# Four feed-forward blocks computed ahead instead of five, with key-sum products and tail remainders moved from VectorE to GpSimd

## The chip, the cores and the metric

The kernel runs on one core of a Trainium2 chip. The metric is the device time of one execution in microseconds. Before the change three runs gave 1642.47, 1645.51 and 1647.66 us; their median is 1645.51 us. The engines are named as in the profile: PE is TensorE (PEld its weight loads), DVE is VectorE, ACT is ScalarE, POOL is GpSimd, SP is SyncE, which here only issues DMAs. A name with q (SPq, POOLq) is that engine's instruction sequencer.

## The reference, cut to what matters

The input x has 2048 rows of 576 numbers in fp32. It is normalised and goes two ways: through a linear attention with 32 heads of 18, and through a gated feed-forward net of width 4608, whose output gates the attention's.

```python
xn = _layernorm(x)                                    # 2048 x 576
q, k, v = split(xn @ wqkv)                            # 32 heads of 18
phi_q = concat(softmax(q @ w_phi), softmax(-(q @ w_phi)))   # phi_k alike
kv = einsum("bhsf,bhsd->bhfd", phi_k, v);  z = einsum("bhsf->bhf", phi_k)
o = einsum("bhqf,bhfd->bhqd", phi_q, kv) / (einsum("bhqf,bhf->bhq", phi_q, z) + 1e-6)
s = o @ wo
g = silu((silu(xn @ w_gate) * (xn @ w_up)) @ w_down)
out = x + s * g
```

All products are made to nearly full fp32 precision: each operand is split into a high part in a reduced fp32 format and a low remainder, and three of the four partial products are added up. ACT casts the high part (line 58) and an elementwise engine subtracts it for the remainder (line 59), so each split costs two elementwise passes.

## The kernel before, in words

The feed-forward width is cut into NF = 36 **F blocks** of 128. The rows of x stay in on-chip memory, transposed, as eight tiles X of 512 columns in two halves (i = 0, 1) of 1024 rows. The work has these stages, told with their places in the profile:

- **Preparation** (0 to about 70 us): load, normalise, transpose and split x, fold w_phi into the query and key weights. 
- **Key stage** (about 70 to 226 us): for each of 16 row tiles, the softmaxes of the keys and the state kv with the key sums z as an extra column, summed in three PSUM banks `kvp` of four, four and two states.
- **Turn to the queries** (lines 492 to 515): ACT copies the ten columns of key sums one at a time from `kvp` into `zc`. Ten small matmuls spread each over 128 rows in PSUM, and four ACT copies gather them in `zb` (lines 501 to 509). Then, for each of the ten states, DVE multiplies by a block mask and the result is split into KVH and KVL (lines 510 to 515).
- **Query stage** (about 226 to 485 us, lines 523 to 636): eight steps of 256 rows. A step has two `q_tile` (projection `pq`, its two softmaxes, and the denominator), one `numer` (transposes of e, product with the states) and one `project` (product with wo, stored to `s_dram`). In `q_tile` DVE multiplies e by `zb` into `ez` (line 568, 1152 columns) and sums by head into y (line 570); y gives the denominator that scales e on line 577. The first use of the buffer `ez` is as a landing place for the last rows of wo (lines 529 to 532), which `split_wo` splits.
- **Tails** (lines 542 to 555, eight calls spread over the query stage): small sums of the last 64 rows of the gate and up weights for later; POOL makes four differences, ACT the high part, DVE the remainder (line 552), and POOL issues twelve DMAs per call to `t_dram`.
- **Main stage** (about 513 us to the end, `gate_up`, line 727 and on): for each half i and each F block not computed ahead, gate and up projections by Strassen's scheme: seven products of seven matmuls (line 706), 512 columns each, which is 49 matmuls per block and half. The down projections (line 805) are interleaved, from a queue that `fill` serves. At its start `operands(0)` loads the row sums that the scheme needs, four tiles of 1280 KB, into the places of x's second half.

The **F blocks computed ahead** (f < EARLY = 5) are made from x directly by `early_tile` (lines 113 to 124), without the scheme: per half two pairs (j = 0, 1) of 2 x 14 matmuls of 512 columns on line 92 (tile `pe`), with a Silu on ACT (line 119) and a product on DVE (line 122). Their result h is stored to `h_dram`, and read back in the main stage by `stored` in place of a `gate_up`. A block is four pairs in all. Two blocks' second halves are made in the preparation, one pair at the end of the key stage, the other pairs of f = 0 to 3 in the query stage as filler between the query's own matmuls, and all of block EARLY - 1 after it (lines 994 to 1000): half 1 before `operands(0)` and half 0 behind it.

The order on each engine is fixed when the kernel is built: a scheduler places each instruction by its place in the program, by what it depends on, and by hints (`high_priority`, `issue_after`). On the chip each engine takes its instructions in that order. `tails(n)` is hinted to come after the e of query tile 3n/2 + 2. In the main stage `units` puts the stored blocks at the places 4f + 1 (first half) and 4f (second half) of the 36.

Of the kernel before, what the change touches and what calls it, by code (L numbers as in the profile page):

```python
# [9 lines left out]
F32 = mybir.dt.float32  # L10
# [3 lines left out]
AX = mybir.AxisListType  # L14
# [3 lines left out]
P = 128  # L18
# [7 lines left out]
GW = GH * DH  # L26
GROUPS = [(g * GW, min(GW, D - g * GW)) for g in range((D + GW - 1) // GW)]
NG = len(GROUPS)
QS = 256
EARLY = 5  # L30
TAILS = (NF - EARLY + 3) // 4
LAG = 3
RUSH = NF - 5
# [4 lines left out]
def heads(ap):  # L38
    return ap.rearrange("p (h d) -> p h d", d=DH)
# [7 lines left out]
def gated_hedgehog_kernel(ctx: ExitStack, tc, x, w_qk, w_v, w_phi, wo, w_gu, w_tail, w_down, ident_in, mask_in, out):  # L47
# [9 lines left out]
    def split(hi, lo, src):  # L57
        nc.scalar.copy(hi, src)  # L58
        nc.vector.tensor_sub(lo, src, hi)  # L59
# [66 lines left out]
    with ExitStack() as att:  # L126
# [364 lines left out]
        with ExitStack():  # L491
            qc = att.enter_context(tc.tile_pool(name="qc", bufs=1, reuse_waits="tile"))
            KVH = qc.tile([GW, 2 * NG, GW], F32R, name="KVH")
            KVL = qc.tile([GW, 2 * NG, GW], F32R, name="KVL")
            zb = qc.tile([P, 2 * D], F32, name="zb")
            zc = qc.tile([GW, 2 * NG], F32, name="zc")
            for i in range(3):
                for j in range(4 if i < 2 else 2):
                    w = GROUPS[(4 * i + j) // 2][1]
                    nc.scalar.copy(zc[0:w, 4 * i + j:4 * i + j + 1], kvp[i][0:w, j, w:w + 1])  # L500
            for s in range(2):
                for a, m, name in ((0, 4, ("p2", "vw")[s]), (4, 1, ("vy", "vx")[s])):
                    o, w = GROUPS[a]
                    zp = kps.tile([P, 512], F32, name=name)
                    for g in range(a, a + m):
                        nc.tensor.matmul(zp[:, (g - a) * GW:(g - a) * GW + w],
                                         zc[0:w, 2 * g + s:2 * g + s + 1].to_broadcast([w, P]), ident[0:w, 0:w],
                                         start=True, stop=True)
                    nc.scalar.copy(zb[:, s * D + o:s * D + o + m * w], zp[:, 0:m * w])
            for i in range(2 * NG):  # L510
                o, w = GROUPS[i // 2]
                km = qc.tile([GW, GW], F32, name="km", bufs=2)
                nc.vector.tensor_mul(km[0:w, 0:w], kvp[i // 4][0:w, i % 4, 0:w],
                                     mask.rearrange("p h d -> p (h d)")[0:w, 0:w])
                split(KVH[0:w, i, 0:w], KVL[0:w, i, 0:w], km[0:w, 0:w])

        raw_x(order[7], 0, 1)
        raw_x(order[7], 2, 3)
# [4 lines left out]
        with ExitStack() as qst:  # L523
# [3 lines left out]
            WOH = qw.tile([GW, NG, D], F32R, name="WOH")  # L527
            WOL = qw.tile([GW, NG, D], F32R, name="WOL")
            wrs = [qk.tile([P, 2, D], F32, name="oh", bufs=1), qk.tile([P, 2, D], F32, name="ol", bufs=1),
                   qk.tile([P, 2, D], F32, name="ez", bufs=1)]  # L530
            for g, (o, w) in enumerate(GROUPS):
                nc.sync.dma_start(wrs[g // 2][0:w, g % 2], wo[o:o + w, :])

# [8 lines left out]
            def tails(n):  # L542
                t = qk.tile([P, 7, P], F32, name="tl", bufs=2)
                hi = qk.tile([P, 7, P], F32R, name="th", bufs=1)
                nc.sync.dma_start(t[:, 0:4], w_tail[n])
                sub = nc.gpsimd.tensor_sub
                sub(t[:, 4], t[:, 2], t[:, 0])
                sub(t[:, 2], t[:, 3], t[:, 2])
                sub(t[:, 5], t[:, 3], t[:, 4])
                sub(t[:, 6], t[:, 1], t[:, 5])  # L550
                nc.scalar.copy(hi, t)
                nc.vector.tensor_sub(t, t, hi)
                for b, src in enumerate((hi.bitcast(F32), hi.bitcast(F32), t)):
                    for q in range(4):
                        nc.gpsimd.dma_start(t_dram[n, q, b], src[32 * q:32 * q + 32])

            last_e = []

            def q_tile(t):
                i0, j0, cols = block(t)  # L560
                pq = qps.tile([P, 2, 512], F32, name="p2")
                for i in range(2):
                    w = slice(i * HALF, (i + 1) * HALF)
                    xw(pq[:, i, 0:HALF], i0, j0, cols, QH[:, :, :, w], QL[:, :, :, w], True)
                e = qk.tile([P, 2 * D], F32, name="e", bufs=4)
                r = softmax_parts(pq, e)
                ez = qk.tile([P, 2 * D], F32, name="ez", bufs=1)
                nc.vector.tensor_mul(ez, e, zb)
                y = qk.tile([P, 2 * H], F32, name="y")
                nc.vector.reduce_sum(y, heads(ez), axis=AX.X)  # L570
                nc.vector.tensor_mul(y, y, r)
                den = qk.tile([P, H], F32, name="den")
                nc.vector.scalar_tensor_tensor(den, y[:, 0:H], DEN_EPS, y[:, H:], op0=ALU.add, op1=ALU.add)
                nc.vector.reciprocal(den, den)
                nc.vector.tensor_mul(r.rearrange("p (s h) -> p s h", s=2), r.rearrange("p (s h) -> p s h", s=2),
                                     den.unsqueeze(1).to_broadcast([P, 2, H]))
                last_e.append(nc.vector.tensor_mul(heads(e), heads(e), spread(r, 2 * H)))
                return e
# [498 lines left out]
```

## Time and profile before

| what | value |
|---|---|
| median of three runs | 1645.51 us |
| the profiled execution's own time | 1645.38 us |
| its span, first to last instruction | 1643.6 us |
| outside the span | 1.8 us |
| instructions | 25222 |
| bytes moved by DMA | 268.47 MB, 163 GB/s on average |

The page of a profile gives busy times of the engines over the whole span. The windows view gives the same for stretches that are named in us from the span's start: of each engine the busy time and, in brackets, the instructions. Groups of instructions are told by line, engine, operation, out<-in by the program's tile names and shape, then the count, the total busy time, the mean of one in ns, and the idle time of the engine just before them with what ended it. The chain of waits follows the work that ended last back to the start. A matmul's duration in a row is longer than its share of the engine, since matmuls overlap: the pace is read from a stretch of many.

### The profile page before, as it was taken

Reading aid. Unit: us, or ns where it says so; the run is one execution under the profiler, and the core shown is the slowest. Engines: PE = TensorE matmul, PEld = TensorE weight load, DVE = VectorE, ACT = ScalarE, POOL = GpSimd, SP = SyncE. Lnnn points to the kernel's source line nnn. Section 1 sums busy time; section 2 is a strip of 40 time slices with the busy share of each in tenths; the row PEclk is TensorE's granted clock in tenths of the full one; section 3 lists DMA queues with packets and bytes.
Section 4 is the critical chain, followed back from the end, with each engine's and each line's share of the span. In section 5 each row is a group of like instructions: output and inputs, shape, how many; then the busy total and the mean of one; then the engine's idle time right before and its main releaser. Section 6 shows DMA issues by size and latency. Waiting matters only on the chain.

```text
span 1643.6 us, 25222 instructions
## 1 busy us (share of the span) xinstructions
PE 1606.3 (98%) x9385; PEld 1428.2 (87%) x9385; DVE 1173.2 (71%) x1733; ACT 723.1 (44%) x1407; POOL 655.0 (40%) x699
## 2 busy tenths in 40 slices
PE   6999999999999999999999999999999999999997
PEld 5899987999987788888888888888888888888886
DVE  7667768989862678788777788825566766666578
ACT  5533344454432554454444444445433433333334
POOL 3385661433213455355445365313243324133132
PEclk9999999999999999999999999999999999999999
DMA  9522243433239545555545554685454655555445
GB/s 293 197 79 78 88 133 114 119 109 110 79 108 329 183 162 172 182 171 177 174 167 181 178 176 156 222 299 157 134 159 138 199 183 172 168 180 182 139 114 173
DMA packets 121741, 268.47 MB, mean 163 GB/s; under 512 B 12786, under 2 KB 53362, under 8 KB 119826
## 3 DMA queue, kind: packets, MB, share of 16 engines
q1 hardware_dynamic: 106652, 246.49, 45.8%
q0 software_dynamic: 3072, 11.02, 2.5%
q10 hardware_dynamic: 11894, 9.35, 1.8%
q8 instruction: 74, 1.21, 0.3%
q14 instruction: 49, 0.40, 0.1%
HBM read 167.19 MB, written 99.61 MB: 162 GB/s over the span
## 4 chain that ended last, share of the span: by engine, by line
PE 66%; DVE 2%; DMA 1%; issue 1%; POOL 0%; ACT 0%; SPq 0%; DVEq 0%; ACTq 0%
PE pd L805 24%; PE px L706 24%; PE pw L706 12%; PE py L706 6%; PE pe L92 1%; DVE acc L777 0%; DVE w L59 0%; DMA rb<-in_B_w_down 0%; DMA ld<-in_B_w_gu 0%; DVE hh L59 0%; DMA X<-s_dram 0%; DVE dw L59 0%; DVE ha L766 0%; DVE acc L778 0%; DVE s L740 0%
## 5 line engine op out<-in xcount | busy, mean ns | idle before, releaser
L805 PEld LDWEIGHTS pd<-dw,hh 128*128 128x128 f32 x3048 | 433.6, 189 | 25.5 <-DVE dw L59 2.0
L805 PE MATMUL pd<-dw,hh 128*128 128x288 f32 x3048 | 449.7, 297 | 3.2 <-DVE dw L59 1.5
L706 PE MATMUL px<-X,w 128*128 128x512 f32 x1488 | 385.9, 393 | 2.1 <-ACT w L58 1.3
L706 PEld LDWEIGHTS px<-X,w 128*128 128x128 f32 x1488 | 270.2, 188 | 55.5 <-ACT s L735 4.0
L706 PE MATMUL pw<-X,w 128*128 128x512 f32 x744 | 191.8, 393 | 0.0
L706 PEld LDWEIGHTS pw<-X,w 128*128 128x128 f32 x744 | 139.1, 188 | 31.2 <-DVE s L740 0.3
L740 DVE TENSOR_TENSOR s<-pw,s 128x512 f32<-128x512 f32 x124 | 85.3, 688 | 103.2 <-ACT s L735 91.7
L930 DVE TENSOR_TENSOR acc<-pd,acc 128x576 f32<-128x576 f32 x128 | 96.3, 753 | 85.3 <-PE pd L805 85.1
L735 ACT COPY s<-px 128x512 f32<-128x512 f32 x124 | 72.6, 586 | 160.0 <-PE px L706 159.9
L92 PE MATMUL pe<-X,wh 128*128 128x512 f32 (+1 forms) x380 | 121.4, 401 | 5.3 <-ACT h L119 2.2
L58 ACT CAST hh<-ha 128x512 fp32r<-128x512 f32 x140 | 82.7, 619 | 92.9 <-PE pd L805 72.6
L59 DVE TENSOR_TENSOR hh<-ha,hh 128x512 fp32r<-128x512 f32 x140 | 109.9, 811 | 18.1 <-ACT hh L58 17.1
L902 POOL TENSOR_TENSOR hb<-hb 128x512 f32<-128x512 f32 x34 | 46.7, 1372 | 161.9 <-DVE hb L762 161.5
L59 DVE TENSOR_TENSOR w<-ld,w 128x512 fp32r<-128x512 f32 (+1 forms) x93 | 79.6, 858 | 37.6 <-ACT w L58 36.3
L706 PE MATMUL py<-X,w 128*128 128x512 f32 x372 | 97.7, 396 | 1.1 <-ACT py L747 1.1
L706 PE MATMUL px<-X,wt 96*128 96x512 f32 x248 | 97.9, 395 | 0.0
L915 POOL TENSOR_TENSOR ha<-ha 128x512 f32<-128x512 f32 x34 | 52.6, 1563 | 104.0 <-DVE hh L59 104.0
L889 POOL TENSOR_TENSOR h<-ha,hb 128x512 f32<-128x512 f32 x34 | 44.9, 1321 | 123.2 <-DVE ha L766 90.1
L58 ACT CAST w<-ld 128x512 fp32r<-128x512 f32 (+1 forms) x93 | 50.9, 549 | 90.1 <-POOL ld L696 58.0
L92 PEld LDWEIGHTS pe<-X,wh 128*128 128x128 f32 (+1 forms) x380 | 69.9, 189 | 20.6 <-DVE h L122 3.4
L693 POOL TENSOR_TENSOR ts<-ld 128x256 f32<-128x256 f32 x31 | 27.3, 880 | 140.7 <-issue 70.0
L747 ACT COPY py<-px 128x512 f32<-128x512 f32 x62 | 35.5, 572 | 103.7 <-PE px L706 84.4
(262 smaller groups left out, 3238.1 us busy)
## 6 DMA issues: line engine op xcount, KB each, us to landing
w_dram<-w SPq DMA_DIRECT2D x90, 512.0 KB, 2.9
w<-w_dram SPq DMA_DIRECT2D x90, 512.0 KB, 4.5
wt<-t_dram SPq DMA_DIRECT2D x61, 336.0 KB, 3.6
ld<-in_B_w_gu SPq DMA_DIRECT2D x31, 512.0 KB, 4.5
X<-sum_dram SPq DMA_DIRECT2D x8, 1280.0 KB, 11.4
rt<-in_B_w_down SPq DMA_DIRECT2D x33, 288.0 KB, 3.0
rb<-in_B_w_down SPq DMA_DIRECT2D x33, 288.0 KB, 4.3
w_dram<-w SPq DMA_DIRECT2D x30, 256.0 KB, 2.2
```

Of the source, the lines that this page charges most:

```text
L58: nc.scalar.copy(hi, src)
L59: nc.vector.tensor_sub(lo, src, hi)
L92: last = nc.tensor.matmul(ps, l, r, start=n == 0, stop=n == len(pairs) - 1)
L706: nc.tensor.matmul(ps, l, r, start=first and n == 0, stop=last and n == len(mm) - 1, skip_group_check=True)
L735: nc.scalar.copy(t, ps)
L740: nc.vector.tensor_add(t, ps, t)
L747: nc.scalar.copy(yp, xp)
L805: nc.tensor.matmul(ps, l, r, start=first and n == 0 and m == 0, stop=n == len(hs) - 1 and m == 2, skip_group_check=True)
L889: sub(s, g["h"][0][0], g["h"][0][1])
L902: nc.gpsimd.tensor_add(a21, a21, g["h"][1][1])
L915: sub(a12, a12, g["h"][0][0])
L930: nc.vector.tensor_add(a2, pd[:, :, 0:HALF], a2)
```

## The change

EARLY falls from 5 to 4, so one F block (four pairs of line 92) is no longer computed ahead and goes through `gate_up` in both halves of the main stage. Four edits in and ahead of the query stage go with it. (1) `ez` is made by POOL in two halves of 576 columns with a buffer each, and DVE sums each half by head. (2) The remainder of the tails is subtracted by POOL instead of DVE, and a tails call issues three DMAs of 128 rows, two from ACT and one from SP, instead of twelve of 32 rows from POOL. (3) The key sums are copied by bank, three ACT copies for ten and two gathering copies for four. (4) The states are masked and split by bank, three times for ten.

```diff
-EARLY = 5
+EARLY = 4
...
-            zc = qc.tile([GW, 2 * NG], F32, name="zc")
-            for i in range(3):
-                for j in range(4 if i < 2 else 2):
-                    w = GROUPS[(4 * i + j) // 2][1]
-                    nc.scalar.copy(zc[0:w, 4 * i + j:4 * i + j + 1], kvp[i][0:w, j, w:w + 1])
-            for s in range(2):
-                for a, m, name in ((0, 4, ("p2", "vw")[s]), (4, 1, ("vy", "vx")[s])):
-                    o, w = GROUPS[a]
-                    zp = kps.tile([P, 512], F32, name=name)
-                    for g in range(a, a + m):
-                        nc.tensor.matmul(zp[:, (g - a) * GW:(g - a) * GW + w],
-                                         zc[0:w, 2 * g + s:2 * g + s + 1].to_broadcast([w, P]), ident[0:w, 0:w],
-                                         start=True, stop=True)
-                    nc.scalar.copy(zb[:, s * D + o:s * D + o + m * w], zp[:, 0:m * w])
-            for i in range(2 * NG):
-                o, w = GROUPS[i // 2]
-                km = qc.tile([GW, GW], F32, name="km", bufs=2)
-                nc.vector.tensor_mul(km[0:w, 0:w], kvp[i // 4][0:w, i % 4, 0:w],
-                                     mask.rearrange("p h d -> p (h d)")[0:w, 0:w])
-                split(KVH[0:w, i, 0:w], KVL[0:w, i, 0:w], km[0:w, 0:w])
+            zc = qc.tile([GW, 12], F32, name="zc")
+            m4 = mask.rearrange("p h d -> p (h d)")
+            banks = [(i, 4 if i < 2 else 2, GROUPS[2 * i][1]) for i in range(3)]
+            for i, n, w in banks:
+                nc.scalar.copy(zc[0:w, 4 * i:4 * i + n], kvp[i][0:w, 0:n, w])
+            zp, zq = kps.tile([P, 2, 512], F32, name="p2"), kps.tile([P, 512], F32, name="vw")
+            for g, (o, w) in enumerate(GROUPS):
+                for s in range(2):
+                    d = zp[:, s, o:o + w] if g < NG - 1 else zq[:, s * w:s * w + w]
+                    nc.tensor.matmul(d, zc[0:w, 2 * g + s:2 * g + s + 1].to_broadcast([w, P]), ident[0:w, 0:w],
+                                     start=True, stop=True)
+            z2, o = zb.rearrange("p (s n) -> p s n", s=2), GROUPS[-1][0]
+            nc.scalar.copy(z2[:, :, 0:o], zp[:, :, 0:o])
+            nc.scalar.copy(z2[:, :, o:D], zq[:, 0:2 * (D - o)].rearrange("p (s n) -> p s n", s=2))
+            for i, n, w in banks:
+                km = qc.tile([GW, 4, GW], F32, name="km")
+                nc.vector.tensor_mul(km[0:w, 0:n, 0:w], kvp[i][0:w, 0:n, 0:w],
+                                     m4[0:w, 0:w].unsqueeze(1).to_broadcast([w, n, w]))
+                split(KVH[0:w, 4 * i:4 * i + n, 0:w], KVL[0:w, 4 * i:4 * i + n, 0:w], km[0:w, 0:n, 0:w])
...
-                   qk.tile([P, 2, D], F32, name="ez", bufs=1)]
+                   qk.tile([P, D], F32, name="ez", bufs=2).unsqueeze(1)]
...
-                nc.vector.tensor_sub(t, t, hi)
+                sub(t, t, hi)
                 for b, src in enumerate((hi.bitcast(F32), hi.bitcast(F32), t)):
-                    for q in range(4):
-                        nc.gpsimd.dma_start(t_dram[n, q, b], src[32 * q:32 * q + 32])
+                    (nc.scalar, nc.scalar, nc.sync)[b].dma_start(t_dram[n, :, b], src)
...
-                ez = qk.tile([P, 2 * D], F32, name="ez", bufs=1)
-                nc.vector.tensor_mul(ez, e, zb)
                 y = qk.tile([P, 2 * H], F32, name="y")
-                nc.vector.reduce_sum(y, heads(ez), axis=AX.X)
+                for s in range(2):
+                    ez = qk.tile([P, D], F32, name="ez", bufs=2)
+                    nc.gpsimd.tensor_mul(ez, e[:, s * D:(s + 1) * D], zb[:, s * D:(s + 1) * D])
+                    nc.vector.reduce_sum(y[:, s * H:(s + 1) * H], heads(ez), axis=AX.X)
```

## The prediction

> **What bounds the kernel now.** First the page: the busy shares and the chain of work that ended last.
>
> ```profile
> PE 1606.3 (98%) x9385; PEld 1428.2 (87%) x9385; DVE 1173.2 (71%) x1733; ACT 723.1 (44%) x1407; POOL 655.0 (40%) x699
> PE 66%; DVE 2%; DMA 1%; issue 1%; POOL 0%; ACT 0%; SPq 0%; DVEq 0%; ACTq 0%
> ```
>
> PE is busy for 98% of the span, and where the chain can be followed it runs through PE. A busy PE need not be a well used one, and the shares are a mean, so the next view is the windows of the stages that the change touches: the query stage in three parts, the turn to the main stage, and a long stretch of the main stage.
>
> ```profile
> core 0: us, PE busy (x) PEld busy (x) DVE busy (x) ACT busy (x) POOL busy (x), PEclk, DMA share, GB/s
> 226.00:270.00 44.00, 39.97 (x223) 34.09 (x221) 33.22 (x60) 23.79 (x47) 18.99 (x28) 1.00 0.49 161
> 270.00:460.00 190.00, 189.00 (x1285) 173.48 (x1286) 171.88 (x266) 85.73 (x151) 55.72 (x112) 1.00 0.34 98
> 460.00:485.00 25.00, 24.54 (x159) 20.81 (x157) 14.03 (x23) 8.68 (x18) 0.00 (x0) 1.00 0.22 67
> 485.00:560.00 75.00, 69.91 (x305) 55.54 (x306) 32.11 (x43) 27.08 (x54) 28.69 (x31) 0.98 0.78 272
> ...
> 226.00:485.00 259.00, 253.51 (x1664) 228.38 (x1662) 219.13 (x347) 118.20 (x215) 74.71 (x140) 1.00 0.35 106
> ...
> 570.00:790.00 220.00, 220.00 (x1233) 195.77 (x1231) 176.20 (x248) 110.40 (x223) 114.80 (x110) 1.00 0.52 175
> ```
>
> The reader is to see that PE is full in the main stage (220.00 of 220) and nearly so in the query stage (253.51 of 259, 5.5 us idle), but that in the middle of the query stage DVE is close behind (171.88 of 190, 90%). There the block computed ahead serves as filler: PE's own query work would finish sooner, and DVE would then set the pace. So a filler block can be taken away profitably only if DVE's load falls with it.
>
> **The block that moves.** The pace of its matmuls is read from the stretch that holds nearly all of the last block, and that of the scheme's from the chain, where a piece of seven matmuls stands alone.
>
> ```profile
> 485.00:520.00 35.00, 24.77 (x104) 19.47 (x104) 2.76 (x4) 2.39 (x4) 1.00 0.91 327
> 564.70 1.63 PE py L706 x7
> L92 PE MATMUL pe<-X,wl 128*128 128x512 f32 x152 | 60.7, 399 | 0.0
> L122 DVE TENSOR_TENSOR h<-pe,h 128x512 f32<-128x512 f32 x11 | 7.6, 690 | 5.7 <-ACT e L282 3.0 <-PE pe L92 2.6
> L63 DVE TENSOR_TENSOR wl<-raw,wh 128x512 fp32r<-128x512 f32 x8 | 5.4, 688 | 6.2 <-ACT wh L62 6.1
> L64 DVE TENSOR_TENSOR wh<-raw,wh 32x256 fp32r<-32x256 f32 x8 | 3.3, 433 | 0.1
> ```
>
> A pair is 28 matmuls, of which eight use `wl`: the 152 in the third row are 19 pairs under `pe` (the twentieth is in other banks), so five blocks of four. The first row, the tile `pe` in this window, gives 24.77/104 = 0.238 us a matmul. One block is 112 matmuls, and **112 x 0.238 = 26.7 us of PE leave** the query stage: the last block still runs behind it, so it is one of the middle that is gone. In the main stage the block costs 2 x 49 matmuls at 1.63/7 = 0.233 us, so **98 x 0.233 = 22.8 us of PE are added**. The main stage is full, so these count whole. Beside them come a weight load, its splits and its stores in the first half and a reload in the second, with the density that 31 such blocks have now while PE is full; for the cover I take nothing more. The stored block that goes had put down-projection work closer together, so DVE's share falls there if anything. **PE's sum is -26.7 + 22.8 = -3.9 us**, if PE stays full in both places.
>
> With the block, DVE loses 4 x 0.69 (line 122) and 2 x (0.69 + 0.43) (lines 63 and 64) = 5.0 us in the query stage.
>
> **The moves off DVE.** These rows are of the query stage's DVE, and below them what POOL does now.
>
> ```profile
> L568 DVE TENSOR_TENSOR ez<-e,zb 128x1152 f32<-128x1152 f32 x16 | 21.3, 1331 | 0.0
> L570 DVE TENSOR_REDUCE y<-ez 128x64 f32<-128x1152 f32 x16 | 21.1, 1317 | 0.0
> L278 DVE TENSOR_REDUCE m<-p 128x32 f32<-128x576 f32 x32 | 23.6, 739 | 0.4 <-PE p L92 0.4
> L552 DVE TENSOR_TENSOR tl<-tl,th 128x896 f32<-128x896 f32 x8 | 8.6, 1080 | 0.0
> core 0: us, POOL busy (x), PEclk, DMA share, GB/s
> 226.00:485.00 259.00, 47.41 (x96) 1.00 0.35 106
> L251 POOL TENSOR_TENSOR KVWL<-wst,KVWH 128x576 fp32r<-128x576 f32 x4 | 6.1, 1542 | 5.0 <-ACT KVWH L249 4.9
> L328 POOL TENSOR_TENSOR slo<-sraw,shi x16: 1281/1497/2448, 107.4 to 237.9; 128x512 fp32r<-128x512 f32 x16
> ```
>
> Off DVE go 21.3 us (`ez`) and 8.6 us (tails). The sum by head in two halves costs 32 x 0.739 (a reduction of 576 columns, line 278) = 23.6 instead of 21.1, so 2.5 us more. POOL gains 32 products of 576 columns: the trace has none, and the nearest is line 251 with 1.54 us, which I take; line 328 scaled by 576/512 bounds it at 1.44 and, at its worst, 2.75. That is 49 us, and 8 remainders of 896 columns at 1.54 x 896/576 = 2.4 us are 19 more. The fifth row (line 555 in the query stage) shows what goes: 96 DMA issues, 47.4 us. POOL ends at about 74.7 - 47.4 + 49 + 19 = 95 us, under half of the stage, so by its sum it does not bound. Sixteen DMA issues go to ACT and eight to SP in place of POOL's 96:
>
> ```profile
> L619 ACTq DMA_DIRECT2D s_dram<-so x32: 326/326/562, 289.9 to 491.2; - x32
> ```
>
> By this row ACT's sixteen are 5 us of a sequencer whose engine is busy for 118 of 259 us. SP's eight wait for POOL's remainder, and what is queued on SP behind them are the stores of h, the next tail and the filler's weights. Those have a step (some 25 us) before they are needed, so I cost this at nothing; without that cover it would be up to eight times a remainder's 2.4 us.
>
> **The turn to the queries.** Ten copies to `zc` become three, ten masks and splits become three.
>
> ```profile
> L513 DVE TENSOR_TENSOR km<-kvp,mask 126x126 f32<-126x126 f32 x8 | 2.1, 283 | 0.7 <-ACT zc L500 0.6
> L59 DVE TENSOR_TENSOR KVL<-km,KVH 126x126 fp32r<-126x126 f32 x8 | 3.9, 502 | 0.7 <-ACT KVH L58 0.7
> 230.77 0.40 PE L92 MATMUL p<-QH,X 128*128 128x288 f32 x1 [1.11 <-ACT zb L509]
> ```
>
> The same columns in fewer instructions cost between nothing and the whole 2.1 + 3.9 = 6.0 us less on DVE; I take 4, since a third of the count is left but each is longer. PE waits 1.11 us here for the last `zb` copy. The copies after the last small matmul become one of about 1000 columns and a short one instead of two, so that wait may go or grow by about as much: I take 0, from -1.1 to +1.1.
>
> DVE in the query stage: 219.1 - 21.3 - 8.6 + 2.5 - 5.0 - 4 = 183 us. PE there: 253.5 - 26.7 = 227 us. DVE's share falls from 85% to about 79%, so the filler that is lost is paid for.
>
> **What POOL's new work costs DVE.** One kind of operation on DVE, with two inputs in on-chip memory and 1152 columns, stands in two stages of the trace: line 409 in the key stage, where POOL computes much, and line 577 in the query stage, where it mostly issues DMAs.
>
> ```profile
> L409 DVE TENSOR_TENSOR phi<-phi,sm x16: 1357/1548/1832, 80.8 to 220.7; 128x1152 f32<-128x1152 f32 x16
> L577 DVE TENSOR_TENSOR e<-e,sm x16: 1345/1358/1360, 269.6 to 465.8; 128x1152 f32<-128x1152 f32 x16
> 220.71 1.81 DVE L409 TENSOR_TENSOR phi<-phi,sm 128x1152 f32<-128x1152 f32 x1
> 221.38 2.28 POOL L328 TENSOR_TENSOR slo<-sraw,shi 128x512 fp32r<-128x512 f32 x1
> ```
>
> Beside POOL's work the median is 0.19 us longer, at worst 0.47, and the last two rows show both slow when they overlap. Sixteen of line 577 and 48 short ones (lines 571, 573, 575) of the kind stand in the stage: 64 x 0.19 = 12 us at most, nothing at least; I take 5, since POOL would compute for a smaller share of this stage than of that one. DVE comes to 188 us, still 39 below PE's 227.
>
> The Trainium skill speaks against this change at this point: SBUF — State Buffer, section "Who interferes with whom", says that a DVE instruction with two inputs in SBUF and a GpSimd instruction that reads SBUF exclude each other, and the second to come waits for the whole of the first. By that rule each of the 64 would wait half a product (0.77 us) in the 40% of the time that POOL computes, an estimate of 64 x 0.77 x 0.4 = 20 us in place of my 5; DVE would then have about 203 us, and the forecast would stand. Row 220.71 agrees in kind: 0.46 us lost, less than a whole instruction of POOL.
>
> **The start of the query stage.** Its idle time on PE stands mostly in the first 45 us.
>
> ```profile
> 256.22 0.50 PE L92 MATMUL pe<-X,wh 128*128 128x512 f32 x1 [0.89 <-ACT h L119]
> 261.47 0.50 PE L92 MATMUL pe<-X,wh 128*128 128x512 f32 x1 [1.71 <-DVE h L122]
> 270.99 0.44 PE L588 MATMUL pt<-ident,e 128*126 128x128 f32 x2 [1.31 <-DVE e L577]
> 256.72 0.75 DVE L59 TENSOR_TENSOR WOL<-ez,WOH 72x576 fp32r<-72x576 f32 x1
> 259.47 1.35 DVE L568 TENSOR_TENSOR ez<-e,zb 128x1152 f32<-128x1152 f32 x1
> ```
>
> PE lives on filler there until the first e is ready at 270.9. The first `ez` starts at 259.47, behind the split of wo's last rows at 256.72, because they lie in the only `ez` buffer. With two buffers the first half need not wait for that, and the first e can come some microseconds sooner; then less filler is eaten at the start and more is left for the steps. The three waits sum to 3.9 us; I take half, **-2 us**, from -3.9 to +2 (a POOL product comes late instead).
>
> **The sum.** 1645.4 (the profiled execution, within 0.2 us of the median of the runs) - 3.9 - 2 = **1639.5 us**, which is 0.36% below. A difference of about 0.3%, 4.9 us, is what a measurement of this kernel can tell from no change.
>
> **The rivals.** (a) PE's sum is right but its idle time doesn't shrink. DVE's lead over PE stays thin in the steps, the scheduler pulls pairs of the last block forward as filler, and their cover is missing where the operands land:
>
> ```profile
> X<-sum_dram SPq DMA_DIRECT2D x8, 1280.0 KB, 11.4
> ```
>
> Between 485 and 520 the DMA engines are at 0.91 (row above) beneath the 104 last matmuls. Each pair pulled forward uncovers up to 28 x 0.238 = 6.7 us. With none to one pair and the idle time as it is: 1641.5 to 1648, typically 1643. For it: PE's idle 5.5 us is small already, and eight matmuls of the last block run early now. Against it: DVE gets lighter.
>
> (b) Slower: **DVE waits for POOL in order**. Line 570 now waits for a product that starts only after the exponential and behind whatever POOL has in front of it, a tails call with 4 differences and a remainder that itself waits for ACT. If DVE waits for each of the 32 products in full, 32 x 1.54 = 49 us join its 188, and the ends of the stage, where DVE is idle anyway (44 - 33.2 and 25 - 14.0, 22 us), come on top: 259 us, as long as now. The block's 22.8 us are added all the same, so 1668. It sets the stage's end once the waits are over 227 - 188 - 22 = 17 us (0.5 us a product), and makes the whole slower than before once the stage is over 259 - 22.8 = 236 us, at waits of 26 us (0.8 us a product); at 1 us a product the stage takes 242, and the time is 1645.4 - 17 + 22.8 = 1651. For it: POOL is slower than DVE for the same columns (2 x 1.54 against 1.33). Against it: the first half can be multiplied while ACT does the second exponential and DVE the sum and reciprocal (lines 285 and 286), so a prompt POOL ends about when DVE is ready. 1650 to 1668, typically 1655.
>
> (c) More than forecast: small stalls between matmuls go too and all 5.5 us of idle vanish, 1645.4 - 3.9 - 5.5 = 1636 or below.
>
> **How the numbers follow.** The forecast (1636.5 to 1642.5) has 0.52, of which 0.38 lies under 1640.6 (0.3% faster); (a) 0.20; (b) 0.18; (c) 0.10. So faster 0.48, within 0.3% 0.34, slower 0.18. The range of 8 in 10 reaches from 1634, which leaves out a part of (c), to 1653, which leaves out the upper part of (b).
>
> **What would show it.** In the profile after, `pe` has 15 pairs and line 706 has 32 x 98 = 3136 matmuls. If I am right, the query stage ends about 28 us sooner (near 457 us), PE idles there 6 us or less, DVE is below 82% and the main stage is about 23 us longer with PE full. If (a) holds, PE idles between the last `pe` and the first line 706 products. If (b) holds, DVE's idle time before line 570 is ended by POOL, and PE idles before line 588. Wrong altogether would be a main stage that grows by more than the block's matmuls.

## The result, and the profile after

The changed kernel takes **1742.23 us** (median of four runs, 1739.66 to 1744.06), the one before 1645.11 us (four runs, 1642.47 to 1647.66): a ratio of 1.0592 with a 95% interval of 1.0572 to 1.0611. That is 97 us slower, where 1639.5 us was forecast and the range ended at 1653. The profiled execution took 1741.55 us, with a span of 1739.8 us.

First the page of the kernel after: busy time of each engine, then tenths of busy time and of granted clock in 40 slices of 43.5 us.

```profile
PE 1628.3 (94%) x9371; PEld 1448.0 (83%) x9371; DVE 1156.1 (66%) x1715; ACT 723.8 (42%) x1397; POOL 672.3 (39%) x647
...
PE   6999977556999899999999999999999999999998
...
PEclk9999998767999999999999999999999999999999
```

PE's share fell from 98% to 94%, and the hole stands in slices 6 to 10, which is the query stage; the granted clock falls there too. The windows of the kernel after, in the stretches that the prediction showed of before, with the main stage at the end:

```profile
core 0: us, PE busy (x) PEld busy (x) DVE busy (x) ACT busy (x) POOL busy (x), PEclk, DMA share, GB/s
226.00:270.00 44.00, 34.88 (x196) 31.17 (x196) 29.16 (x38) 17.57 (x25) 20.83 (x24) 0.88 0.50 160
270.00:460.00 190.00, 123.27 (x691) 112.12 (x690) 84.19 (x144) 52.50 (x89) 47.01 (x46) 0.78 0.23 77
460.00:485.00 25.00, 24.26 (x168) 22.26 (x168) 21.93 (x37) 7.92 (x17) 5.68 (x4) 1.00 0.08 29
485.00:560.00 75.00, 73.66 (x507) 67.06 (x506) 59.75 (x100) 32.86 (x60) 14.21 (x10) 1.00 0.20 67
...
586.00:1739.00 1153.00, 1139.81 (x6186) 998.56 (x6184) 795.24 (x1134) 507.62 (x993) 448.90 (x403) 1.00 0.54 177
```

Between 270 and 460 PE issued 691 matmuls; before it was 1285. From 460 on the pace is back, with POOL nearly idle. The query stage ran late and everything behind it ran at its old pace. How much was lost, and to what, comes from one window of each kernel, from 226 us to its first matmul of the scheme. Before, then after:

```profile
226.00:512.90 286.90, 280.44 (x1784) 250.21 (x1783) 225.63 (x356) 124.42 (x227) 83.99 (x151) 1.00 0.41 128
```

```profile
226.00:586.10 360.10, 279.60 (x1672) 251.53 (x1672) 199.33 (x324) 115.97 (x201) 90.92 (x88) 0.87 0.29 96
```

The 112 matmuls of the block are gone, as they should be (1784 - 1672), and the stretch is 73.2 us longer all the same. PE's idle time grew from 6.5 to 80.5 us, which is 74.0. Its busy time stayed where it was, though 112 x 0.238 = 26.7 us of work went: what was left took 25.9 us longer. That goes with the granted clock of 0.87. Between 270 and 460 us a matmul of 512 columns (line 92, `pe<-X,wh`) took 473 ns in the mean, and 399 before. Thus 74.0 + 25.9 - 26.7 = 73.2. The main stage runs from 512.9 to 1643.6 before (1130.7 us) and from 586.1 to 1739.8 after (1153.7 us): 23 us more. 73 + 23 are the 96 us of the span.

What was waited for, in the kernel after from 226 to 485 (engine, line, what for: us in total, times, longest), first the engines, then SP's own queue:

```profile
POOL tl L546 <- DMA tl<-in_B_w_tail: 70.9, 5, 17.3
POOL ez L568 <- ACT e L282: 70.1, 11, 25.3
DVE y L569 <- POOL ez L568: 51.9, 10, 14.7
ACT th L550 <- DMA t_dram<-th: 48.6, 5, 15.6
PEld p L613 <- ACT so L617: 40.6, 9, 12.1
...
ACT so L617 <- DMA s_dram<-so: 20.5, 2, 12.2
```

```profile
SPq L544 <- DMA t_dram<-tl: 79.2, 6, 15.5
```

The reader is to look for the lines that no other engine explains. ACT waits 48.6 us at the cast of the tails (line 550), and what it waits for is a store: `th` has one buffer, and the stores of the tail before must have read it. SP waits 79.2 us for the store of `tl` before it loads the next one. The other lines follow: POOL waits for the tail that SP has not loaded and for the e of an ACT that stands at line 550; DVE waits for POOL, PE for ACT. One such event, from the timeline of ACT in the kernel after:

```profile
292.40 0.53 ACTq L553 DMA_DIRECT2D t_dram<-th  x1
...
294.08 0.53 ACTq L553 DMA_DIRECT2D t_dram<-th  x1
...
298.81 0.38 ACT L58 CAST oh<-po 126x256 fp32r<-126x256 f32 x1
311.19 0.94 ACT L550 CAST th<-tl 128x896 fp32r<-128x896 f32 x1 [11.99 <-DMA t_dram<-th]
```

Two stores of 448 KB, issued at 292.4 and 294.1, let go of `th` at 311.2. ACT stood idle for 12 us before it, and PE for 9.5 us up to 312.9, at line 613:

```profile
312.93 0.61 PE L613 MATMUL p<-WOH,oh 126*128 126x288 f32 x1 [9.53 <-ACT oh L58]
```

In the DMA view of that time, 300 to 340 us in 40 slices, the busy share of the 16 engines in tenths and what they moved:

```profile
DMA  2222222211104773122222222222211631223522
GB/s 104 104 104 108 90 90 104 93 47 50 54 11 43 221 303 47 25 65 92 82 115 100 100 108 108 100 108 108 93 50 50 111 152 29 39 29 89 168 94 100
```

While the stores run, about a quarter of the DMA engines is busy (a share of 0.26 from 300 to 308 us in the windows view), at about 100 GB/s; other traffic in the same view reaches 0.7 and 303 GB/s. At 104 GB/s two stores of 458,752 bytes take 8.8 us, and three, with SP's store of `tl`, 13.2; the rest of the 17 us is not followed here. So the first theory, **S**: the new stores of 128 rows into `t_dram[n, :, b]`, a destination whose slowest dimension has four entries, are slow, and in-order queues carry that to PE. The rivals were: the stores are slow because ACT and SP issue them (**I**); POOL's new work makes DVE late by itself (**P**, rival (b) of the prediction); the filler block is missing (**F**).

### The profile page after: what moved, and what is told of

Its sections match the earlier page's. It is cut to its first block, busy times and chain, and to the rows that moved or that the text cites. A ratio compares the mean times of both kernels' runs of the same rounds, so it can differ in the third digit from the quotient of the medians.

```text
span 1739.8 us, 25112 instructions
## 1 busy us (share of the span) xinstructions
PE 1628.3 (94%) x9371; PEld 1448.0 (83%) x9371; DVE 1156.1 (66%) x1715; ACT 723.8 (42%) x1397; POOL 672.3 (39%) x647
## 4 chain that ended last, share of the span: by engine, by line
PE 63%; DVE 1%; issue 0%; DMA 0%; ACT 0%; DVEq 0%; SPq 0%
PE px L705 23%; PE pd L804 23%; PE pw L705 11%; PE py L705 6%; DVE acc L776 0%; DMA X<-s_dram 0%; DVE hh L59 0%; DVE ha L765 0%; DVE acc L777 0%; DVE dw L59 0%; DVE s L739 0%; DVE acc L959 0%; DVE w L59 0%; DVE X L929 0%; DVE acc L929 0%
## 5 line engine op out<-in xcount | busy, mean ns | idle before, releaser
L804 PEld LDWEIGHTS pd<-dw,hh 128*128 128x128 f32 x3048 | 434.0, 189 | 25.9 <-DVE dw L59 2.2
L705 PE MATMUL px<-X,w 128*128 128x512 f32 x1536 | 398.5, 394 | 3.9 <-ACT s L734 2.9
L705 PEld LDWEIGHTS px<-X,w 128*128 128x128 f32 x1536 | 279.1, 188 | 59.6 <-ACT s L734 6.6
L705 PE MATMUL pw<-X,w 128*128 128x512 f32 x768 | 198.3, 393 | 0.0
L705 PEld LDWEIGHTS pw<-X,w 128*128 128x128 f32 x768 | 143.5, 188 | 32.3 <-DVE s L739 0.3
L92 PE MATMUL pe<-X,wh 128*128 128x512 f32 x300 | 101.5, 416 | 7.5 <-ACT h L119 5.8
L613 PE MATMUL p<-WOH,oh 126*128 126x288 f32 (+1 forms) x160 | 54.4, 341 | 55.7 <-ACT so L617 38.5
L568 POOL TENSOR_TENSOR ez<-e,zb 128x576 f32<-128x576 f32 x32 | 45.2, 1421 | 122.3 <-ACT e L282 118.5
L613 PEld LDWEIGHTS p<-WOH,oh 126*128 126x128 f32 (+1 forms) x160 | 33.5, 209 | 64.2 <-ACT so L617 42.9
```

Source lines behind the costliest of these rows:

```text
L92: last = nc.tensor.matmul(ps, l, r, start=n == 0, stop=n == len(pairs) - 1)
L568: nc.gpsimd.tensor_mul(ez, e[:, s * D:(s + 1) * D], zb[:, s * D:(s + 1) * D])
L613: nc.tensor.matmul(ps[:, 0:HALF], a[0:w, g, jc], bw[0:w, g, n], start=k == 0, stop=k == 3 * NG - 1)
L705: nc.tensor.matmul(ps, l, r, start=first and n == 0, stop=last and n == len(mm) - 1, skip_group_check=True)
L804: nc.tensor.matmul(ps, l, r, start=first and n == 0 and m == 0, stop=n == len(hs) - 1 and m == 2, skip_group_check=True)
```

## The experiments

**The shape of the stores, each way.** In `e3_rows32` only the shape goes back to twelve stores of 32 rows; ACT and SP still issue them. In `e1_pool_issue` POOL issues them too. In `e2_before_three` the kernel before gets the three stores of the change.

```diff
e3: +for q in range(4): (nc.scalar, nc.scalar, nc.sync)[b].dma_start(t_dram[n, q, b], src[32*q:32*q+32])
e1: +for q in range(4): nc.gpsimd.dma_start(t_dram[n, q, b], src[32*q:32*q+32])
e2 (on before): +(nc.scalar, nc.scalar, nc.sync)[b].dma_start(t_dram[n, :, b], src)
```

> The changed kernel, its tails stored by twelve transfers of 32 rows that ACT (eight) and SP (four) issue. Same queues and bytes as the change, another shape. Theory S with the shape as its cause (the destination's outer dimension is 4): each lands in 2 to 4 us as POOL's did, and the time is 1636 to 1650 us, with 8 x 0.34 us of issuing on ACT for each tail. Theory S with the queue as its cause (ACT and SP share theirs with other transfers): the stores stay slow, over 1700 us. Rivals P and F: over 1700 us.

> The changed kernel, but the tails are stored as before the change, by twelve transfers of 32 rows from POOL. Theory S (the three new stores of 128 rows each take some 9 us to land and hold ACT and SP, and nearly all of the 97 us comes from that): 1636 to 1648 us, no stalls of 8 to 12 us on PE before line 613. Rival P (DVE waits for POOL's products, my rival b): still over 1700 us, since the products stay on POOL. Rival F (four blocks are too little filler): still over 1700 us.

> The kernel before with one edit alone: its tails are stored by the three transfers of 128 rows, two from ACT and one from SP. Everything else, five blocks and the products on DVE, is as before. Theory S: 1645 + 60 to 100 = 1705 to 1745 us, with ACT waiting for t_dram at the tails' cast. Rivals P and F: 1640 to 1650 us, since POOL has less to do than before and the filler is all there.

Beside a before of 1643.16 us: `e3_rows32` 1651.64 us (ratio 1.0049, 1.0034 to 1.0064), `e1_pool_issue` 1659.39 us (1.0096, 1.0081 to 1.0111), `e2_before_three` 1672.62 us in its one run. Of the 97 us, 89 went with the shape alone and 81 where POOL issued besides; and the shape alone costs the kernel before 29 us. `e3_rows32` lies just above what S allowed, the other two clearly outside. The same window of `e3_rows32`:

```profile
270.00:460.00 190.00, 185.71 (x1297) 173.95 (x1296) 162.96 (x268) 85.91 (x153) 66.78 (x55) 1.00 0.38 106
```

1297 matmuls instead of 691, at a full clock. S stands in kind, and I falls. But 8 us are left over before, where a gain was forecast, and 29 us is far from 97: something makes S dearer in the changed kernel.

**Another cure of the same stores.** `e5_layout` keeps three stores of 128 rows, but lays `t_dram` out so that each is one run of 128 rows; the loads in the main stage become three for one.

```diff
+t_dram tile [TAILS, 3, P, 7, P]; store to t_dram[n, b]
+for b in range(3): nc.sync.dma_start(wt.bitcast(F32)[32*b:32*b+32], t_dram[n, b, 32*q:32*q+32])
```

> The changed kernel, with the tails' buffer in DRAM laid out by part and then by all 128 rows, so that each of the three stores goes to one run of 128 rows; three loads of 32 rows replace the one of 96 in the main stage. Number, queues and bytes of the stores are those of the change. Theory S with the shape as cause: the stores land in 2 to 4 us and the time is 1636 to 1648 us. With the size of a transfer or the queue as cause: over 1700 us. The loads cost two more issues of 0.35 us on SP per block, hidden.

It took 1665.45 us (1.014, 1.0123 to 1.0157), so the expectation failed. The stores themselves are cured. The rows of the tile `t_dram` in the kernel after (issues of ACT: ns min/median/max, first to last start), then in `e5_layout`:

```profile
L553 ACTq DMA_DIRECT2D t_dram<-th x16: 525/525/638, 251.6 to 398.4; - x16
```

```profile
L553 ACTq DMA_DIRECT2D t_dram<-th x16: 326/326/444, 252.4 to 330.1; - x16
```

An issue takes 326 instead of 525 ns, the median store lands after 2.6 us (DMA view, 280 to 320), and the busy share of the DMA engines goes to 0.9 there:

```profile
DMA  0000644988809896912807377075000400899910
GB/s 0 0 0 0 276 183 197 401 319 201 313 10 380 344 401 253 209 68 104 355 0 308 151 316 290 0 199 211 0 0 0 148 0 0 316 358 393 401 57 14
...
t_dram<-th ACTq DMA_DIRECT2D x8, 448.0 KB, 2.6
```

The Trainium skill has the rule for it: DMA: Bandwidth & Descriptors, section "Why a DMA increments its semaphore by 16 and not by 1", says that a DMA goes to the largest number of engines, up to 16, that divides the slowest dimension of both its sides, and that hardware queues take the lowest numbered ones. With a slowest dimension of four, that is four engines, the same for every such store: 4 of 16 is a share of 0.25, and the kernel after shows 0.26 from 300 to 308 us.

The second row shows something else: all sixteen stores are issued between 252 and 330 us, though the tails are meant to be spread over the stage. In the query stage, PE loses its time up to the end of that stretch (windows of `e5_layout`):

```profile
226.00:270.00 44.00, 35.24 (x203) 31.44 (x203) 30.77 (x38) 20.72 (x29) 29.72 (x31) 0.88 0.57 197
270.00:340.00 70.00, 62.72 (x415) 56.80 (x414) 57.39 (x94) 33.00 (x54) 38.86 (x37) 1.00 0.48 177
340.00:460.00 120.00, 118.65 (x835) 109.59 (x834) 99.00 (x167) 48.93 (x94) 22.78 (x16) 1.00 0.08 28
```

**The hint that lost its holder.** That led to a second theory, **H**. `tails(n)` is held back by `issue_after` on the `e` of a query tile, an instruction of DVE. If the hint only orders instructions of that engine, it held the tails by their one DVE instruction, the remainder, which POOL now has: nothing paces them. The order in the timelines fits. In the kernel before, DVE's eight remainders stand behind the e of query tile 3, 4, 6, 7, 9, 10, 12 and 13 (counted from 1), as the hint names them, while POOL takes the differences of the first two calls from 250 us on, before any e is finished. In the changed kernel the differences of the eight calls stand behind 1, 2, 3, 5, 6, 8, 8 and 10 of POOL's 32 products; had the hint held them, it would be 6, 8, 12, 14, 18, 20, 24 and 26.

`e5_layout` has exactly the order of the changed kernel. It differs in the layout and the loads that go with it, so the slow stores are worth 75 of the 97 us where the calls come this early (1742.23 to 1665.45 us, each beside its own before). In `e3_rows32` the differences stand behind 1, 2, 3, 8, 12, 16, 18 and 22 products: with the other shape the builder also spread the calls, and the 89 us hold some of that. At the start POOL still takes the differences of the first call between the two halves of the first product. From the timeline of POOL in `e3_rows32`:

```profile
238.89 1.44 POOL L569 TENSOR_TENSOR ez<-e,zb 128x576 f32<-128x576 f32 x1 [1.02 <-ACT e L282]
247.73 0.45 POOL L546 TENSOR_TENSOR tl<-tl 128x128 f32<-128x128 f32 x1 [7.39 <-DMA tl<-in_B_w_tail]
...
249.62 1.40 POOL L569 TENSOR_TENSOR ez<-e,zb 128x576 f32<-128x576 f32 x1
```

POOL waits 7.4 us for a tail's load with the second half queued behind it; PE's first projection after it, in the timeline of the same kernel, comes after 9.29 us of nothing:

```profile
258.30 0.58 PE L92 MATMUL p<-QH,X 128*128 128x288 f32 x1 [9.29 <-DVE e L279]
```

`e10_anchor` is `e3_rows32` with the hint tied to POOL's second product of the same tile, `e11_anchor_slow` the changed kernel with only that. `e6_ez_dve` takes P's test: `e3_rows32` with product and sum back on DVE as before, in one buffer `ez` (the diffs are shortened).

```diff
e10, e11: -tc.issue_after(last_e[3 * n // 2 + 2].ins)
e10, e11: +tc.issue_after(last_z[2 * (3 * n // 2 + 2) + 1].ins)   # last_z: the products on POOL
e6: -for s in range(2): nc.gpsimd.tensor_mul(ez, ...) ; nc.vector.reduce_sum(...)
e6: +nc.vector.tensor_mul(ez, e, zb); nc.vector.reduce_sum(y, heads(ez), axis=AX.X)
```

> The changed kernel with the stores in 32 rows from ACT and SP, and the tails' hint tied to POOL's second product of query tile 3n/2 + 2 in place of DVE's e. Theory H (the hint holds back only instructions of its own engine, and the change left no tails instruction on DVE, so POOL takes the first tails between the first tile's two products and waits there for their load): the 9.5 us stall of PE near 249 us and the low clock behind it are gone, and the time is 1634 to 1642 us. Rival P (POOL's products themselves come too late for DVE): the stall stays or moves, 1648 to 1654 us, as with the unpaced tails (1651.6).

> The changed kernel with its three stores of 128 rows, and only the hint tied to POOL's product. If slow stores and lost pacing multiply each other (unpaced, all eight tails run back to back and each holds the single cast buffer for some 20 us, so that ACT is blocked most of the time): paced tails cost about what the slow stores cost the kernel before (1672.6 - 1643.2 = 29 us), so 1660 to 1685 us. If the slow stores alone explain the time: 1720 us or more.

> The changed kernel with the stores in 32 rows, and the products and sums by head of key sums back on DVE as before the change (one buffer, 1152 columns); tails and their remainders stay on POOL, unpaced. Theory H: DVE no longer stands behind the first tails' load, the 9.5 us stall is gone, DVE has 19 us more work: 1640 to 1650 us. If the stall comes from somewhere else in the start of the query stage: 1652 us or more.

Beside a before of 1644.84 us: `e10_anchor` 1646.83 us (1.0014, 1.0005 to 1.0024), `e11_anchor_slow` 1702.84 us (1.0351, 1.0333 to 1.0369), `e6_ez_dve` 1649.1 us (1.0031, 1.0016 to 1.0047). In `e10_anchor` and `e11_anchor_slow` the differences stand behind products 6, 8, 12, 14, 18, 20, 24 and 26, the very ones that the hint names: in this builder the hint orders its own engine's instructions alone, and H is shown.

`e11_anchor_slow` lies between its two expectations and meets neither. Pacing alone takes 39 of the 97 us off and leaves 58; the shape alone takes 89 off and leaves 8; both leave 2. The two thus overlap: each costs more beside the other. Why 58 are left, where the same stores cost the kernel before 29, is not fully shown. At the tails' cast ACT waits no longer than in `e2_before_three` (18.3 and 20.2 us, 226 to 500 us), but at `so` (line 617) it waits 43.6 us for the stores to `s_dram`, and 16.7 there.

In `e10_anchor` POOL's first two products stand next to each other, as its timeline shows, but the second still waits 4.1 us for DVE, and the time missed its expectation by 5 us:

```profile
239.65 1.43 POOL L569 TENSOR_TENSOR ez<-e,zb 128x576 f32<-128x576 f32 x1 [1.35 <-ACT e L282]
245.18 1.43 POOL L569 TENSOR_TENSOR ez<-e,zb 128x576 f32<-128x576 f32 x1 [4.11 <-DVE y L570]
```

`e6_ez_dve` says about P that the products on POOL are no large cost: with them gone the stall at the start is gone too (PE is busy for 39.97 of the 44 us from 226 to 270, as before), and 1649.1 against 1651.64 us is 0.18%, with intervals that overlap.

**Where the last two microseconds are.** `e12_early5_paced` is `e10_anchor` with five blocks, for F: if the missing block costs, it must be faster.

```diff
-EARLY = 4
+EARLY = 5
```

> As e10_anchor (stores of 32 rows from ACT and SP, tails tied to POOL's product), but with five blocks ahead, so that only the block's move is undone. Theory F (with the faults mended, what is left over is filler: four blocks are one too few for the query stage, its last block is eaten as filler and PE idles for DVE's and POOL's answers): the query stage's idle time on PE falls from some 11 us to under 5, and the time is 1639 to 1644 us, below e10. Rival N (the block's move gives its 3.9 us and the rest of the loss lies in POOL's and ACT's new work): 1647 to 1652 us, above e10.

It took 1651.84 us (1.0052, 1.0037 to 1.0067, beside 1643.95), slower than `e10_anchor`. F falls. The relief itself then loses time, also with five blocks. The waits of `e12_early5_paced` from 226 to 485 name a place:

```profile
POOL tl L551 <- ACT th L550: 11.1, 5, 4.5
...
PE pt L588 <- DVE e L577: 6.4, 4, 2.3
```

POOL's remainder (line 551) waits up to 4.5 us for ACT's cast, and the products queued behind it make e late. `e17_rem_dve` is `e10_anchor` with the remainder back on DVE, `e19_early5_rem_dve` the same with five blocks, `e18_before_rows32` the kernel before with its twelve stores issued by ACT and SP.

```diff
e17, e19: -sub(t, t, hi)
e17, e19: +nc.vector.tensor_sub(t, t, hi)
e18 (on before): -nc.gpsimd.dma_start(t_dram[n, q, b], src[32 * q:32 * q + 32])
e18 (on before): +(nc.scalar, nc.scalar, nc.sync)[b].dma_start(t_dram[n, q, b], src[32 * q:32 * q + 32])
```

> As e10_anchor (four blocks, paced tails, stores of 32 rows), with the tails' remainder back on DVE. If POOL's remainders, 2.1 us each between its products, delay the denominators: 1640 to 1645 us. If DVE's 8.6 us are worth more: 1648 to 1653 us.

> Five blocks, products on POOL, stores of 32 rows from ACT and SP, tails tied to POOL's product, remainder on DVE; e12 without its remainder on POOL. If POOL's products cost the 8 us: 1650 to 1653 us, as e12. If the remainder on POOL costs them: 1642 to 1646 us.

> The kernel before with its twelve stores per tail issued by ACT (eight) and SP (four) instead of POOL, same shape. If the residue lies in the stores on ACT's queue, where ACT then waits for them: 1648 to 1652 us. If it lies in POOL's products or remainders: 1642 to 1645 us, as before.

Beside a before of 1645.27 us: `e17_rem_dve` **1642.71 us** (0.998, 0.997 to 0.9989), `e19_early5_rem_dve` 1643.49 us (0.9985, 0.9976 to 0.9994), `e18_before_rows32` 1643.79 us (0.9988, 0.9975 to 1.0001). So the remainder on POOL costs 0.67% with five blocks (1.0052 to 0.9985) and 0.34% with four (1.0014 to 0.998). `e18_before_rows32` and `e2_before_three` differ in the shape of the stores alone, 1643.79 against 1672.62 us. In `e19_early5_rem_dve` the wait at line 551 is gone and PE's is down to a quarter:

```profile
PE pt L588 <- DVE e L577: 1.7, 2, 1.1
```

`e17_rem_dve` has the lowest median of the study, 2.6 us below the kernel before beside it; the intervals of these three overlap. Its stretch from 270 to 460 has 184.64 of 190 us with a matmul, where `e10_anchor` has 180.42:

```profile
270.00:460.00 190.00, 184.64 (x1284) 172.72 (x1283) 165.74 (x270) 84.98 (x150) 56.56 (x59) 1.00 0.41 114
```

```profile
270.00:460.00 190.00, 180.42 (x1251) 168.11 (x1250) 152.68 (x250) 83.44 (x148) 76.11 (x66) 1.00 0.41 115
```

**All stores on SP.** If issues on ACT were a cost, moving them to SP would show it: `e14_sp_stores` is `e10_anchor` with all stores from SP, `e15_early5_sp` the same with five blocks.

```diff
-(nc.scalar, nc.scalar, nc.sync)[b].dma_start(t_dram[n, q, b], ...)
+nc.sync.dma_start(t_dram[n, q, b], ...)
```

> As e10_anchor with four blocks, but all twelve stores of 32 rows of a tail are issued by SP and none by ACT. In e10 ACT waited 10 us for its own queue of stores. If these waits reach PE: 1638 to 1643 us. If they are hidden, or SP's queue holds up the loads behind them instead: 1645 to 1650 us.

> Both: five blocks ahead and all stores of the tails from SP, paced by POOL's product. The sum of the two gains if there are any: 1636 to 1642 us, faster than the kernel before. Without any: 1644 to 1650 us.

They took 1664.06 us (1.0122, 1.0106 to 1.0137) and 1664.66 us (1.0131, 1.0114 to 1.0148), beside 1643.95: both expectations failed. That of `e14_sp_stores` had named SP's queue as what could hold things up, and put it at 1650 us at most. SP's own waits in `e14_sp_stores` from 226 to 560:

```profile
SPq L554 <- ACT so L618: 41.8, 3, 20.7
SPq L662 <- PE pe L92: 35.8, 4, 16.7
SPq L554 <- DMA s_dram<-so: 32.7, 10, 9.8
SPq L554 <- ACT oh L58: 28.9, 3, 15.0
```

SP stands at a tail's store until ACT has come to the cast, up to 20.7 us, and what is queued on SP behind it waits too. The scheme's first product starts at 513.2 us, where it starts at 493.1 in `e10_anchor`; the way from SP to PE was not followed further.

**The block alone, and the banks alone.** `e7_early4_only` is the kernel before with EARLY = 4 and nothing else; `e16_banks` the kernel before with edits (3) and (4), key sums and masked states by bank.

```diff
e7 (on before): -EARLY = 5
e7 (on before): +EARLY = 4
e16 (on before): the hunk of the change from zc to the split by bank, as printed above
```

> The kernel before with four blocks ahead for five and nothing else. If DVE would set the query stage's pace without its relief, as the prediction said: DVE has 219 - 5 = 214 us and 40 us of idle time at the ends and between, so the stage shrinks by about 5 of the 26.7 us, and the time is 1655 to 1665 us. If the relief wasn't needed: 1638 to 1646 us.

> The kernel before with the key sums and the masked states by bank (the third and fourth edit) and nothing else. The prediction took 4 us less of DVE and nothing on PE for these, from -1.1 to +1.1: 1644 to 1646 us, with the query's first product starting between 1 us sooner and 1 us later than at 230.8 us. If they loosen the start of the query stage further: 1640 to 1643 us.

`e7_early4_only` took 1655.05 us (1.007, 1.0046 to 1.0093, beside 1644.84), `e16_banks` 1643.74 us (0.9993, 0.9984 to 1.0002, beside 1643.95). The block must not be taken away without the relief. The last block was pulled forward as filler: the last matmul of `pe` starts at 479.7 us (the row of line 92 in `e7_early4_only`), 15 us before the scheme's first product, where before it is 0.4 us. Nothing is left to fill the last steps of the queries, and PE is busy for 9.07 of the 15 us from 480 to 495. It isn't the operands that it waits for: their first load is issued at 385.7 us, before at 496.6. The row, and the window in which the main stage starts:

```profile
L92 PE MATMUL pe<-X,wh x300: 389/396/646, 20.6 to 479.7; 128*128 128x512 f32 x120, 96*128 96x512 f32 x30
```

```profile
465.00:540.00 75.00, 62.25 (x292) 49.81 (x292) 34.08 (x49) 26.97 (x54) 25.39 (x27) 0.89 0.54 183
```

## Why the prediction was wrong, step by step

- **What bounds the kernel**: right for the main stage, where PE is busy for 1117.1 of 1130.7 us before and 1139.7 of 1153.7 after. In the query stage the prediction had PE as the bound, with 227 us of work against DVE's 188; there the waits of the queues for one another set the length.
- **The block that moves**: right in size. The 112 matmuls left the query stage, 3136 went through line 705, and the main stage grew by 23 us (22.8 forecast). Its worth, forecast as -3.9 us (0.24%), was 0.38% with the remainder on POOL (`e12_early5_paced` to `e10_anchor`) and 0.05% with it on DVE (`e19_early5_rem_dve` to `e17_rem_dve`), where the intervals overlap: with the relief in order, it is hardly worth anything that these runs can tell. From `e19_early5_rem_dve` to `e17_rem_dve` the scheme's first product comes 23.5 us sooner (514.4 to 490.9), not 26.7, and the main stage behind it takes 24.3 us more.
- **The moves off DVE, the issue of the stores: the step that failed.** The prediction put it as "Sixteen DMA issues go to ACT and eight to SP ... By this row ACT's sixteen are 5 us of a sequencer", and SP's eight "have a step (some 25 us) before they are needed, so I cost this at nothing". It priced a store by its issue, from the row of another store, and not by its time on the DMA engines, nor by what holds `th` until it has ended. By the runs the shape costs 29 us alone (`e2_before_three`, one run), 89 of the 97 us here (after to `e3_rows32`), and 75 where the order of the calls stays the same (after to `e5_layout`). For SP "nothing" would have needed the next tail's load not to be behind the store: SP waited 79.2 us there.
- **The same step, the remainder moved**: priced as 19 us of work on a POOL with room, which it is (2.09 us each, 2.4 forecast), but it also was what the hint held on to. Nothing in the prediction spoke of the pacing. It is worth 39 us with slow stores (after to `e11_anchor_slow`) and about 6 us without (`e3_rows32` to `e10_anchor`, 0.35%), though there the calls were spread in part already. And its place in POOL's queue, behind ACT's cast and ahead of the products, costs 0.34 to 0.67% more.
- **Prices on POOL and DVE**: right. Groups of the kernel after (count, busy us, mean ns, idle before):

```profile
L568 POOL TENSOR_TENSOR ez<-e,zb 128x576 f32<-128x576 f32 x32 | 45.2, 1421 | 122.3 <-ACT e L282 118.5 <-ACT so L617 3.9
L569 DVE TENSOR_REDUCE y<-ez 128x32 f32<-128x576 f32 x32 | 23.6, 736 | 55.2 <-POOL ez L568 55.0
L551 POOL TENSOR_TENSOR tl<-tl,th 128x896 f32<-128x896 f32 x8 | 16.7, 2088 | 27.9 <-ACT th L550 27.9
```

  The product takes 1.42 us (1.54 forecast), the half sum 0.736 us (0.739), the remainder 2.09 us.
- **What POOL's work costs DVE**: 5 us was taken, 12 at most. The median of line 577 hides it (1358 ns in `e10_anchor` as before), the mean doesn't. The two rows that grew most, before and then in `e10_anchor`, 226 to 485 us:

```profile
L577 DVE TENSOR_TENSOR e<-e,sm 128x1152 f32<-128x1152 f32 x16 | 21.7, 1355 | 0.3
L575 DVE TENSOR_TENSOR sm<-sm,den 128x64 f32<-128x64 f32 x16 | 3.5, 216 | 0.3
```

```profile
L577 DVE TENSOR_TENSOR e<-e,sm 128x1152 f32<-128x1152 f32 x16 | 26.3, 1641 | 0.3
L575 DVE TENSOR_TENSOR sm<-sm,den 128x64 f32<-128x64 f32 x16 | 6.4, 401 | 0.2
```

  With lines 571 and 573 the four groups take 9.6 us more in `e10_anchor` and 6.0 in `e17_rem_dve`, so the price was of the right size. The 20 us that the prediction worked out from the Trainium skill's page is about twice the larger of these.
- **The turn to the queries**: right, 0 (`e16_banks`, whose interval includes 1).
- **The start of the query stage**: half right. The first `ez` no longer waits for wo, and the first e comes sooner: line 577 starts at 257.1 in `e10_anchor` and at 269.6 before. The -2 us was not seen. In the kernel after PE stalls at the same place, with the tails in POOL's queue (row below, from PE's timeline). In `e10_anchor`, without tails there, PE still idles for 4.3 of the 44 us from 226 to 270, and 4.0 before.

```profile
259.42 0.58 PE L92 MATMUL p<-QH,X 128*128 128x288 f32 x1 [9.12 <-DVE e L279]
```
- **The rivals**: (b) named the right kind of loss, DVE behind POOL in order, and gave it 1655 and at most 1668; its price per product was bounded by a product's 1.54 us, while DVE in fact waited 51.9 us for ten products, up to 14.7 for one, since POOL was itself held up by a DMA. Of (a), `e7_early4_only` shows the last block eaten as filler, but not the operands' landing, whose loads were issued early there. No rival had a store that is slow or a tail that comes early, and so the range ended 89 us too low.

What stays open: `e5_layout` and `e1_pool_issue` lose more than `e3_rows32` (22 and 16 us against 8). For `e5_layout` the early order of the calls, shown above, is a likely cause, not tested alone; its three loads for one in the main stage may be another, since that stage takes 1157.8 us against 1154.6. In `e1_pool_issue` POOL has 96 issues beside its products; its share was not measured alone. Nor are the 58 us of `e11_anchor_slow` explained in full. A second buffer for `th`, which would take ACT's wait away and leave the slow store, was not tried.

## What to carry to other kernels

Price a DMA that is given a new shape by its time on the engines and by the buffer that it holds, not by its issue; fewer and larger isn't faster when the slowest dimension becomes small. When an instruction changes its engine, look for what depended on its being where it was: a hint, an order in a queue, the engine that paces the rest. And take a bundle of edits apart before judging its idea: here the whole, mended, was worth 0.2% (`e17_rem_dve`), its block nothing that the runs can tell, and one line of it cost 75 to 89 us. A median can hide a cost that only some of the instructions pay: read the mean beside it.

## What the hardware showed that was not expected

The stores of 448 KB with four entries in their slowest dimension kept the DMA engines at a share of 0.26 and about 100 GB/s, and an issue took 525 ns on ACT's sequencer. In one run of 128 rows an issue was 326 ns, and the DMA engines moved up to 401 GB/s with such stores and other loads in flight.

Idle time on PE was paid for twice here: where PE stalled for 9 us and more at a time, the granted clock was 0.78 (270 to 460 us) and the same matmul of 512 columns took 473 instead of 399 ns. By the windows above that is 26 us beside the 74 us of idle time.
